# Items of 608 slots instead of 640 in a routed mixture of experts, with places turned into items by comparisons

## The chip, the core and the metric

The program runs on one core of one Trainium2 chip. Its time is the device time of one execution in microseconds (us); the figure that is compared is the median of several executions. TensorE (PE) does the matrix products, VectorE (DVE), ScalarE (ACT) and GpSimd (POOL) the element-wise work, and the queues of SyncE (SP), ACT and POOL issue transfers (DMA).

## The reference, cut to what matters

Three layers follow one another. A linear attention over 4 batches of 576 positions gives 2,304 rows of 512 numbers. A dense layer of hidden width 1,024 with a softmax gate and a norm turns each row into another row `x` of 512. Then a mixture of eight experts takes each row to the one expert with the largest logit:

```python
logits = x @ w_gate
e_idx = np.argmax(logits, axis=1)
...
for e in range(E):                      # E = 8, x is 2304 x 512
    mask = e_idx == e
    if not mask.any():
        continue
    h = np.maximum(x[mask] @ w1[e], 0.0)    # 512 -> 1024
    ye = h @ w2[e]                          # 1024 -> 512
    out[mask] = gate_w[mask, None] * eom[mask, e, None] * ye
```

How many rows an expert gets is known only when the logits are. Everything is float32. The kernel keeps that precision by splitting each operand of the large products into a high and a low half (type fp32r) and adding three products: high by high, high by low, low by high.

## The kernel before, in words

**Tokens.** The 2,304 rows are 18 tiles of 128. For each tile a list of short steps is written (`kp`, `ha`, `ub` and so on), and a long list called `ORDER` fixes by hand the order in which the steps of all tiles are issued. Within that list every instruction of an engine is tied to the one before it on the same engine, so PE, DVE, ACT, POOL and SP each go strictly in the listed order. Behind the list, in the stage of the experts, only PE's order is fixed (`in_turn`); the order on DVE, ACT and POOL is made by a planner that simulates the program when it is built.

**Places.** When the logits of some tiles are there, routing is done for a set of tiles at once (`SETS`: four, four, four, three, two and one tiles, numbered 0 to 5). Step `ra` finds the expert of each token, `rc` and the step `re` (L714 to L745) count how many tokens of the same expert came earlier. That count is the token's `place`. `re` splits it by shift and mask into a block of 128 (`col`) and a lane (`flo`). All of it is DVE work on tiles of 128 by one to four numbers, and each instruction needs the result of the one before. Then `rf` computes the token's weight, `rg` builds for each tile a one-hot matrix of lanes (`ea`) and one of blocks (`er`), and `rh` multiplies the two on PE into a table `tab`: for each expert and each of its blocks, which token sits in which lane. Sets 0 to 4 are in `ORDER`; set 5 is issued behind it, by `rest`.

**Items.** `CAP` = 640 slots make one item: five blocks of 128 (`NBLK`), all of one expert. An expert with more tokens than `CAP` gets further items (up to `NSURE` = 4 of them have columns in the table). Slots without a token are computed too, and their rows are not written. The first `NSURE` = 4 items are always done, unrolled; items beyond that are done in a conditional `body` behind them, if there are any.

For an item, `fetch` gathers rows of `x` by an indirect transfer for each block (L803) and loads the expert's weights. `xpose` transposes the blocks on PE (L158), and ACT and DVE write the high and low halves `xt`. `up` forms the hidden layer: for each of eight groups of 128 hidden units twelve products (four pieces of the width of 512, three each) with a weight block held in PE and the item's slots streaming past. A product streams at most 512 columns, so the slots go in two parts: 256 and 384 for the first item (`up` with `at` 0 and `CA * P`), 320 and 320 for the others. ACT and DVE turn the result into halves `ht` (L929, L930). `down` takes block by block: the block's 128 slots of `ht` are held in PE, and the 512 columns of `w2` stream past, 24 products a block. ACT scales the result (L951), and an indirect transfer scatters the rows to the output (L952).

While an item runs, the weights of the next are loaded and split into halves on ACT, POOL and DVE (`split_behind`), and its blocks are transposed between the products of the last two blocks of `down`. For the first item, two blocks are prepared early (`zg`, `zt`, `zh`, `zs`, inside `ORDER`), and the other three are gathered during its `down` of the first two blocks (`first_item`, L803) and transposed at product group 4 of the second.

All matrix products are recorded at L155, all transposes at L158.

Of the kernel before, what the change touches and what calls it, by code (L numbers as in the profile page):

```python
# [22 lines left out]
F32 = mybir.dt.float32  # L23
F32R = mybir.dt.float32r
I32 = mybir.dt.int32
AF = mybir.ActivationFunctionType
ALU = mybir.AluOpType
# [4 lines left out]
P = 128  # L32
# [4 lines left out]
DM = H * D  # L37
NPAIR = H // 2
# [1 line left out]
NF = F // P  # L40
E = 8
EF = 1024
CAP = 640
NBLK = CAP // P
LT = 4
QA = 3
DF = 4
# [5 lines left out]
NSURE = -(-NT // CAP)  # L53
# [3 lines left out]
NB = NSURE * NBLK  # L57
NR = E * NB
BIG = 8192.0

# [51 lines left out]
def moe_kernel(ctx: ExitStack, tc: tile.TileContext, qT, kT, v, bd, w_in, w_out, g_wg,  # L114
               w1, w2, ident_in, numbers, out):
    nc = tc.nc
# [4 lines left out]
    x2d = dram.tile([NT, DM], F32, name="x2d")  # L121

    ident = cst.tile([P, P], F32, name="ident")
# [26 lines left out]
    def in_turn(ins):  # L150

        return tc.keep_in_program_order(ins) if fixed[0] else ins
# [2 lines left out]
        return in_turn(nc.tensor.matmul(ps, **kw))  # L155

    def transpose(ps, x):
        return in_turn(nc.tensor.transpose(ps, x, ident))  # L158

    def mm3(ps, lh, ll, rh, rl, first, last):  # L160
        mm(ps, lhsT=lh, rhs=rh, start=first, stop=False)
        mm(ps, lhsT=lh, rhs=rl, start=False, stop=False)
        mm(ps, lhsT=ll, rhs=rh, start=False, stop=last)

    with ExitStack() as ab:
# [548 lines left out]
        def re(i):  # L714

            a, z, n, r = named(i)
            d = of["r", i]
            seen = d["seen"]

            base = r("base", [P, 2 * E])  # L720
            V.tensor_copy(out=base, in_=d["pps"])
            total = rt.tile([P, E], F32, tag="total", name=f"total_{a}", bufs=2)
            if count[0] is None:
                V.tensor_copy(out=total, in_=base[:, E:2 * E])
            else:
                V.tensor_tensor(out=total, in0=count[0], in1=base[:, E:2 * E], op=ALU.add)
                V.tensor_tensor(out=base[:, 0:E], in0=base[:, 0:E], in1=count[0], op=ALU.add)
            count[0] = total
            V.tensor_tensor(out=seen, in0=seen, in1=base[:, 0:E].unsqueeze(2).to_broadcast([P, E, n]), op=ALU.add)
            V.tensor_tensor(out=seen, in0=seen, in1=d["oh"], op=ALU.mult)  # L730
            place = r("place", [P, n])
            V.reduce_sum(out=place, in_=seen.rearrange("p e t -> p t e"), axis=AX.X)
            V.tensor_scalar(out=place, in0=place, scalar1=-1.0, scalar2=None, op0=ALU.add)
            pli = r("pli", [P, n], I32)
            V.tensor_copy(out=pli, in_=place)
            plh = r("plh", [P, n], I32)
            V.tensor_scalar(out=plh, in0=pli, scalar1=7, scalar2=None, op0=ALU.arith_shift_right)
            V.tensor_scalar(out=pli, in0=pli, scalar1=127, scalar2=None, op0=ALU.bitwise_and)
            col = d["col"] = r("col", [P, n])
            V.tensor_copy(out=col, in_=plh)  # L740
            flo = d["flo"] = r("flo", [P, n])
            V.tensor_copy(out=flo, in_=pli)

            V.scalar_tensor_tensor(out=col, in0=d["em"][:, :, 0], scalar=-float(NB), in1=col, op0=ALU.mult, op1=ALU.add)
            V.tensor_scalar(out=col, in0=col, scalar1=float(E * NB), scalar2=None, op0=ALU.add)  # L745
# [54 lines left out]
            return o[:, 0:k, 0:b]  # L800

        def gather(x, j, col, n=NT):
            return nc.gpsimd.indirect_dma_start(out=x[:, j, :], out_offset=None, in_=x2d[0:n, :],  # L803
                                                in_offset=bass.IndirectOffsetOnAxis(ap=col, axis=0),
                                                bounds_check=n - 1, oob_is_err=False)

        def load_expert(raw, src, at, eng=nc.sync):
# [20 lines left out]

        def xpose(x, xt, blocks, name):
            for j in blocks:  # L830
                ps = sm.tile([P, NPAIR, P], F32, tag="sm", name=f"xT{name}_{j}")
                for c in range(NPAIR):
                    transpose(ps[:, c, :], x[:, j, c * P:(c + 1) * P])
                hi, lo = (y[:, :, j * P:(j + 1) * P] for y in xt)
                nc.scalar.copy(out=hi, in_=ps)  # L835
                sub(nc.vector, lo, ps, hi)

# [102 lines left out]

    def down(i, ht, blocks, between={}):
        for j in blocks:
            ps = psy.tile([P, DM], F32, tag="psy", name=f"yp{i}_{j}")
            for f in range(EF // P):
                if (j, f) in between:
                    between[j, f]()
                mm3(ps, ht[0][:, f, j * P:(j + 1) * P], ht[1][:, f, j * P:(j + 1) * P],
                    w2h[:, f, :], w2l[:, f, :], f == 0, f == EF // P - 1)
            y = cp.tile([P, DM], F32, tag="y", name=f"y{i}_{j}", bufs=3)
            col = i * NBLK + j  # L950
            nc.scalar.activation(out=y, in_=ps, func=AF.Copy, scale=scs[:, col:col + 1])  # L951
            nc.gpsimd.indirect_dma_start(out=out, out_offset=bass.IndirectOffsetOnAxis(ap=idxs[:, col:col + 1], axis=0),  # L952
                                         in_=y, in_offset=None, bounds_check=NT - 1, oob_is_err=False)

    def new_x(i):
# [193 lines left out]
```

## Time and profile before

| | |
|---|---|
| time, median of 3 runs | 661.83 us (661.37 to 673.13) |
| the profiled execution | 665.99 us, of which its span is 664.3 us |
| granted TensorE clock, mean over the span | 0.983 |
| PE busy | 639.2 us (96% of the span), 4,434 products |
| PE weight loads | 582.0 us (88%) |
| DVE, ACT, POOL busy | 358.8 us, 296.7 us, 163.8 us |
| DMA | 55.22 MB, mean 83 GB/s |

The span runs from the first to the last instruction of the program; times inside it are counted from its start. Products on PE are pipelined: the record of one shows its whole passage, which overlaps the next, so the cost of a product in a stream is the distance from its start to the next start and not its duration. The stage of the experts' items begins at about 417 us; the last 240 us or so are `up` and `down`. The groups of rows on which the prediction rests stand in a section of their own below.

### The profile page before, as it was taken

How to read it: one execution, taken by the hardware profiler on the slowest of the kernel's cores; microseconds unless marked ns; L12 is line 12 of the kernel's file. 1: busy time of each engine (PE TensorE's matmuls, PEld its weight loads, DVE VectorE, ACT ScalarE, POOL GpSimd, SP SyncE). 2: the span in 40 equal slices, each digit the busy share in tenths (PEclk: the TensorE clock that was granted, in tenths of full speed). 3: DMA queues.
4: the chain of work that ended last, by engine and by line, in shares of the span. 5: the costliest groups of instructions: out<-in, count | busy, mean ns of one | idle time of the engine just before them, and what ended most of it. 6: DMA issues, size and time to landing. Idle time of an engine off the chain costs nothing. (4 is left out here: it accounts for less than half of the span.)

```text
span 664.3 us, 11388 instructions
## 1 busy us (share of the span) xinstructions
PE 639.2 (96%) x4434; PEld 582.0 (88%) x4434; DVE 358.8 (54%) x1010; ACT 296.7 (45%) x719; POOL 163.8 (25%) x133
## 2 busy tenths in 40 slices
PE   9988999999999999999999989899999999999995
PEld 8988898899998999889889879779899889889984
DVE  5999977555455446756587586883523222422200
ACT  5677646446435644635424354422443233324210
POOL 1344423111012001110012115044590355216011
PEclk9979969999999999999999999999999999999999
DMA  8952402022210510100000301428542433010001
GB/s 293 303 156 96 143 2 64 1 67 79 65 33 1 159 33 2 33 17 28 6 1 18 143 32 51 156 86 313 181 129 78 165 114 127 17 47 9 1 33 42
DMA packets 35199, 55.22 MB, mean 83 GB/s; under 512 B 2624, under 2 KB 21440, under 8 KB 35137
## 3 DMA queue, kind: packets, MB, share of 16 engines
q1 hardware_dynamic: 28384, 31.73, 14.8%
q0 software_dynamic: 6464, 22.55, 10.0%
q8 instruction: 37, 0.61, 0.4%
q14 instruction: 26, 0.20, 0.1%
q10 hardware_dynamic: 288, 0.13, 0.1%
HBM read 44.96 MB, written 9.96 MB: 83 GB/s over the span
## 5 line engine op out<-in xcount | busy, mean ns | idle before, releaser
L155 PE MATMUL x<-w2h,lth 128*128 128x256 f32 (+1 forms) x288 | 83.8, 291 | 1.4 <-DVE xr L485 1.3
L155 PE MATMUL x<-w2l,lth 128*128 128x256 f32 (+1 forms) x288 | 81.9, 284 | 0.0
L155 PE MATMUL x<-w2h,ltl 128*128 128x256 f32 (+1 forms) x288 | 81.9, 284 | 0.0
L930 DVE SCALAR_TENSOR_TENSOR htl<-hp,hth 128x320 fp32r<-128x320 f32 (+2 forms) x64 | 31.4, 491 | 87.3 <-ACT hth L929 76.8
L558 POOL TENSOR_SCALAR s<-s,st 128x1024 f32<-128x1024 f32 x18 | 23.3, 1294 | 201.9 <-DVE st L554 93.4
L155 PE MATMUL hp<-xth,w1h 128*128 128x320 f32 (+1 forms) x224 | 70.3, 314 | 0.9 <-DVE htl L930 0.9
L155 PE MATMUL hp<-xtl,w1h 128*128 128x320 f32 (+1 forms) x224 | 70.2, 313 | 0.0
L155 PE MATMUL hp<-xth,w1l 128*128 128x320 f32 (+1 forms) x224 | 70.1, 313 | 0.0
L155 PE MATMUL yp<-w2h,hth 128*128 128x512 f32 x160 | 64.2, 401 | 0.0
L155 PE MATMUL yp<-w2l,hth 128*128 128x512 f32 x160 | 63.2, 395 | 0.0
L155 PE MATMUL yp<-w2h,htl 128*128 128x512 f32 x160 | 63.0, 393 | 0.0
L929 ACT ACTIVATE hth<-hp 128x320 fp32r<-128x320 f32 (+2 forms) x64 | 28.1, 439 | 74.4 <-PE hp L155 74.2
L155 PE MATMUL h<-w1h,xth 128*128 128x512 f32 x144 | 58.9, 409 | 0.0
L155 PE MATMUL h<-w1l,xth 128*128 128x512 f32 x144 | 56.9, 395 | 0.0
L155 PE MATMUL h<-w1h,xtl 128*128 128x512 f32 x144 | 56.9, 395 | 0.0
L155 PEld LDWEIGHTS x<-w2h,lth 128*128 128x128 f32 x288 | 54.1, 188 | 2.9 <-issue 1.5
L155 PEld LDWEIGHTS x<-w2l,lth 128*128 128x128 f32 x288 | 54.2, 188 | 0.3
L155 PEld LDWEIGHTS x<-w2h,ltl 128*128 128x128 f32 x288 | 54.3, 189 | 0.0
L525 DVE TENSOR_REDUCE st<-h 128x1 f32<-128x512 f32 x36 | 24.8, 689 | 45.2 <-PE h L155 45.2
L143 DVE TENSOR_TENSOR xtl<-xT,xth 128x512 fp32r<-128x512 f32 x36 | 24.7, 687 | 40.7 <-ACT xth L835 38.2
L372 ACT ACTIVATE qe<-qps,qmx 128x128 f32<-128x128 f32 x144 | 39.0, 392 | 17.1 <-DVE qmx L365 17.1
L951 ACT ACTIVATE y<-yp,scs 128x512 f32<-128x512 f32 x20 | 13.8, 690 | 69.3 <-PE yp L155 61.0
(200 smaller groups left out, 1469.7 us busy)
## 6 DMA issues: line engine op xcount, KB each, us to landing
raw<-in_w POOLq DMA_DIRECT2D x12, 1024.0 KB
v<-in_v SPq DMA_DIRECT2D x18, 260.0 KB, 4.2
kr<-in_kT SPq DMA_DIRECT2D x18, 256.0 KB, 4.5
qr<-in_qT SPq DMA_DIRECT2D x18, 256.0 KB, 4.2
x2d<-xo SPq DMA_DIRECT2D x18, 256.0 KB, 2.0
win<-in_w_in SPq DMA_DIRECT2D x8, 512.0 KB, 7.7
wout<-in_w_out SPq DMA_DIRECT2D x8, 512.0 KB, 3.6
raw<-in_w SPq DMA_DIRECT2D x4, 1024.0 KB, 6.3
```

The lines of the kernel that those rows point to most:

```text
L143: return eng.tensor_tensor(out=out_, in0=a, in1=hi.bitcast(F32), op=ALU.subtract)
L155: return in_turn(nc.tensor.matmul(ps, **kw))
L372: nc.scalar.activation(out=e3[:, 2 * c + j, :], in_=pss[j][:, c, :], func=AF.Exp, bias=nmx[:, j, c:c + 1])
L525: nc.vector.tensor_reduce(out=st[:, n:n + 1], in_=of[f"h{n}", t], axis=AX.X, op=ALU.max, negate=True)
L558: nc.gpsimd.tensor_scalar(out=s, in0=s, scalar1=st[:, 10:11], scalar2=st[:, 11:12], op0=ALU.mult, op1=ALU.add)
L929: act = nc.scalar.activation(out=hi, in_=ps[:, 0:n], func=AF.Relu)
L930: dve = nc.vector.scalar_tensor_tensor(out=lo, in0=ps[:, 0:n], scalar=0.0, in1=hi.bitcast(F32), op0=ALU.max, op1=ALU.subtract)
L951: nc.scalar.activation(out=y, in_=ps, func=AF.Copy, scale=scs[:, col:col + 1])
```

## The change

An item has 608 slots, 19 times 32, instead of 640. There are still five blocks, but the last one holds 96 slots. A new function `slots(j)` gives a block's length, and the gathers, the transposes, the products of `down`, the scaling and the scatters of the last block use 96 partitions or columns instead of 128. In `up` the parts are 256 and 352 for the first item and 304 and 304 for the others. The number of items that are always done (`NSURE`), of items at most (`NITEM`) and of columns in the table (`NR`) come out as before: 4, 11 and 160.

Since a block in the table still has 128 lanes, item k of an expert begins at place 640 k in the table, though its first token is the expert's token 608 k. So 32 is added to a place for each item boundary that it has passed. `re` does that with the place divided by 32: three instructions, one for each k from 1 to 3, compare it with 20 k - 1 and add the comparison's result (1 or 0). The scaling by 1/32 goes into an instruction that was there, and the scaling back replaces a copy.

```diff
-CAP = 640
-NBLK = CAP // P
+CAP = 608
+NBLK = -(-CAP // P)
+SHORT = NBLK * P - CAP
...
+def slots(j):
+    return min(P, CAP - j * P)
...
     def transpose(ps, x):
-        return in_turn(nc.tensor.transpose(ps, x, ident))
+        k = x.shape[0]
+        return in_turn(nc.tensor.transpose(ps, x, ident[0:k, 0:k]))
...
-            V.tensor_scalar(out=place, in0=place, scalar1=-1.0, scalar2=None, op0=ALU.add)
+            V.tensor_scalar(out=place, in0=place, scalar1=-1.0, scalar2=1.0 / SHORT, op0=ALU.add, op1=ALU.mult)
+            for k in range(1, NSURE):
+                V.scalar_tensor_tensor(out=place, in0=place, scalar=float(k * (CAP // SHORT + 1) - 1), in1=place,
+                                       op0=ALU.is_ge, op1=ALU.add)
             pli = r("pli", [P, n], I32)
-            V.tensor_copy(out=pli, in_=place)
+            V.tensor_scalar(out=pli, in0=place, scalar1=float(SHORT), scalar2=None, op0=ALU.mult)
...
         def gather(x, j, col, n=NT):
-            return nc.gpsimd.indirect_dma_start(out=x[:, j, :], out_offset=None, in_=x2d[0:n, :],
-                                                in_offset=bass.IndirectOffsetOnAxis(ap=col, axis=0),
+            k = slots(j)
+            return nc.gpsimd.indirect_dma_start(out=x[0:k, j, :], out_offset=None, in_=x2d[0:n, :],
+                                                in_offset=bass.IndirectOffsetOnAxis(ap=col[0:k], axis=0),
...
         def xpose(x, xt, blocks, name):
             for j in blocks:
-                ps = sm.tile([P, NPAIR, P], F32, tag="sm", name=f"xT{name}_{j}")
+                k = slots(j)
+                ps = sm.tile([P, NPAIR, P], F32, tag="sm", name=f"xT{name}_{j}")[:, :, 0:k]
                 for c in range(NPAIR):
-                    transpose(ps[:, c, :], x[:, j, c * P:(c + 1) * P])
-                hi, lo = (y[:, :, j * P:(j + 1) * P] for y in xt)
+                    transpose(ps[:, c, :], x[0:k, j, c * P:(c + 1) * P])
+                hi, lo = (y[:, :, j * P:j * P + k] for y in xt)
...
     def down(i, ht, blocks, between={}):
         for j in blocks:
-            ps = psy.tile([P, DM], F32, tag="psy", name=f"yp{i}_{j}")
+            k = slots(j)
+            ps = psy.tile([P, DM], F32, tag="psy", name=f"yp{i}_{j}")[0:k]
...
-                mm3(ps, ht[0][:, f, j * P:(j + 1) * P], ht[1][:, f, j * P:(j + 1) * P],
+                mm3(ps, ht[0][:, f, j * P:j * P + k], ht[1][:, f, j * P:j * P + k],
                     w2h[:, f, :], w2l[:, f, :], f == 0, f == EF // P - 1)
-            y = cp.tile([P, DM], F32, tag="y", name=f"y{i}_{j}", bufs=3)
+            y = cp.tile([P, DM], F32, tag="y", name=f"y{i}_{j}", bufs=3)[0:k]
             col = i * NBLK + j
-            nc.scalar.activation(out=y, in_=ps, func=AF.Copy, scale=scs[:, col:col + 1])
-            nc.gpsimd.indirect_dma_start(out=out, out_offset=bass.IndirectOffsetOnAxis(ap=idxs[:, col:col + 1], axis=0),
+            nc.scalar.activation(out=y, in_=ps, func=AF.Copy, scale=scs[0:k, col:col + 1])
+            nc.gpsimd.indirect_dma_start(out=out, out_offset=bass.IndirectOffsetOnAxis(ap=idxs[0:k, col:col + 1], axis=0),
                                          in_=y, in_offset=None, bounds_check=NT - 1, oob_is_err=False)
```

## Rows read from the trace of the kernel before

**Rows 1.** The page: busy time by engine, and the granted clock in 40 slices.
```profile
PE 639.2 (96%) x4434; PEld 582.0 (88%) x4434; DVE 358.8 (54%) x1010; ACT 296.7 (45%) x719; POOL 163.8 (25%) x133
...
PEclk9979969999999999999999999999999999999999
```

**Rows 2.** Windows: window, length, busy of PE, PEld, DVE, ACT, POOL, clock, DMA.
```profile
440.00:640.00 200.00, 198.17 (x1125) 179.75 (x1124) 62.48 (x106) 68.05 (x113) 79.94 (x59) 1.00 0.31 105
```

**Rows 3.** Waits of PE: who waited for whom, total us, times, longest us.
```profile
PE tab L155 <- DVE er L770: 2.8, 3, 1.4
```

**Rows 4.** Groups by line and form, PE: count, busy us, mean ns, idle before.
```profile
L155 PE MATMUL hp<-xth,w1h 128*128 128x320 f32 x192 | 59.5, 310 | 0.9 <-DVE htl L930 0.9
...
L155 PE MATMUL kv<-v,ke 128*128 128x65 f32 x256 | 30.7, 274 | 0.0
...
L155 PE MATMUL kv<-v,ke 64*128 64x65 f32 x64 | 9.1, 300 | 0.0
```

**Rows 5.** Timeline of PE (start us, duration us): first and last of three streams.
```profile
305.90 0.28 PE L155 MATMUL x<-w2h,lth 128*128 128x256 f32 x1
...
308.63 0.28 PE L155 MATMUL x<-w2h,ltl 128*128 128x256 f32 x1
...
600.58 0.31 PE L155 MATMUL hp<-xth,w1h 128*128 128x320 f32 x1
...
628.73 0.40 PE L155 MATMUL yp<-w2h,hth 128*128 128x512 f32 x1
...
656.29 0.40 PE L155 MATMUL yp<-w2h,htl 128*128 128x512 f32 x1
```

**Rows 6.** Timeline of DVE and PE, set 3 of the routing; idle before in brackets.
```profile
391.14 0.17 DVE L733 TENSOR_SCALAR place<-place 128x3 f32<-128x3 f32 x1
391.35 0.17 DVE L735 CAST pli<-place 128x3 int32<-128x3 f32 x1
...
394.76 0.71 DVE L770 SCALAR_TENSOR_TENSOR er<-nums,col,tsc 128x480 fp32r<-128x480 f32 x1
...
395.53 0.71 PE L155 MATMUL tab<-er,ea 128*128 128x480 f32 x2 [1.36 <-DVE er L770]
```

**Rows 7.** Timeline of DVE and PE behind set 4, where the items begin.
```profile
419.12 0.69 DVE L143 TENSOR_TENSOR xtel<-xTe,xteh 128x512 fp32r<-128x512 f32 x1
...
419.86 0.39 PE L155 MATMUL hp<-xtel,w1h 128*128 128x256 f32 x1 [2.32 <-DVE xtel L143]
```

**Rows 8.** Timeline of DVE and PE behind set 2.
```profile
345.38 0.71 DVE L770 SCALAR_TENSOR_TENSOR er<-nums,col,tsc 128x480 fp32r<-128x480 f32 x1
...
346.42 0.38 PE L155 MATMUL tab<-er,ea 128*128 128x480 f32 x1
```

**Rows 9.** Timeline of DVE behind sets 0 and 1, idle before in brackets.
```profile
274.38 0.69 DVE L525 TENSOR_REDUCE st<-h 128x1 f32<-128x512 f32 x1 [0.57 <-PE h L155]
...
311.43 0.69 DVE L143 TENSOR_TENSOR ltl<-lT,lth 128x512 fp32r<-128x512 f32 x1 [3.35 <-ACT lth L586]
```

**Rows 10.** Timeline of DVE and PE behind set 5.
```profile
431.04 0.71 DVE L770 SCALAR_TENSOR_TENSOR er<-nums,col,tsc 128x480 fp32r<-128x480 f32 x1
...
434.45 0.38 PE L155 MATMUL tab<-er,ea 128*128 128x480 f32 x1
```

**Rows 11.** Timeline of POOL and PE: the first item's last gather and its transposes.
```profile
439.91 1.00 POOL L803 DMA_INDIRECT xg<-x2d,idxg  x1 [0.30 <-issue]
...
443.72 0.63 PE L158 MATMUL xT<-ident,xg 128*128 128x128 f32 x4 [0.97 <-DVE idxg L984]
```

**Rows 12.** The last scatter: POOL's timeline, then the DMA view 657.7:664.3 (packets, MB).
```profile
657.79 0.98 POOL L952 DMA_INDIRECT out_y<-y,idxs  x1 [4.63 <-ACT y L951]
...
q0 software_dynamic: 80, 0.10, 4.7%
```

**Rows 13.** Windows, columns as in the second group: one at half clock, one around 419.86.
```profile
82.00:95.00 13.00, 12.75 (x65) 12.17 (x66) 9.99 (x29) 7.12 (x18) 1.30 (x1) 0.50 0.07 24
...
412.00:422.00 10.00, 7.68 (x66) 7.47 (x65) 8.24 (x56) 2.75 (x9) 0.00 (x0) 1.00 0.55 201
```

## The prediction

> **What bounds the kernel now.** I read the page first. PE is busy for 639.2 us of a span of 664.3, no other engine for more than 54% of it, and outside two early dips the granted clock is full [rows 1]. In the stage of the items the window view says the same more sharply: 198.17 of 200 us [rows 2]. So time falls there only by what leaves PE's own stream, and time rises wherever PE is made to wait longer. The waits of PE say where it waits for DVE on the way to the items: three times for the one-hot matrix `er` of the routing, 2.8 us together [rows 3], and once, for 2.32 us, for the low half of the first item's transposed rows [rows 7]. Those are the places where added DVE work can show.
>
> What a product costs PE I take from starts in undisturbed streams, not from the records' durations [rows 5]. 24 products of 256 columns start from 305.90 to 308.63, 23 steps of 118.7 ns. 192 of 320 columns start from 600.58, and what follows them starts at 628.73: 146.6 ns. 120 of 512 columns start from 628.73 to 656.29, 119 steps of 231.6 ns. Between 256 and 320 columns that is 0.436 ns a column, between 320 and 512 it is 0.443. I take 0.44.
>
> **The products of `up`.** Items 1 to 3 have 576 products in all of 320 columns (three operand pairs, one row each of 192 [rows 4]); each loses 16. The first item has 96 of 384 columns; each loses 32. That is 576 x 16 + 96 x 32 = 12,288 columns, at 0.44 ns **5.4 us less** (5.36 to 5.44 by the two slopes). All of it lies on PE's path, because PE stands still for 1.83 of 200 us there [rows 2]. ACT and DVE, busy for about a third of that window, have shorter operands to evict and nothing more to do. The weights' splits get 1.35 us less cover per `up`; POOL, the busiest of them, has 120 of 200 us idle there, so I cost that at nothing (if that cover fails, at most the same 1.35 us per item comes back, 5.4 in all).
>
> One rule can be set beside this. The Trainium skill, "TensorE: Matmul & The Clock Gate", section "Back-to-back issue gap", gives the distance of warm products as the columns at 2.4 GHz plus about 2.5 ns. By it 320 columns would take 135.8 ns, where this trace has 146.6, and the 12,288 columns would be worth 5.1 us, an estimate from that page, so that the whole sum would come out 0.3 us smaller.
>
> **The last block in `down`.** The number of products stays at 24 a block, 96 for the four last blocks, and the streamed operand stays at 512 columns; only the held one has 96 columns instead of 128. In rows 5 the distance follows the streamed columns with 128 held throughout; a product with 96 held is in no row. If the held share counted fully, 96 products would lose a quarter of 231.6 ns: 5.6 us of gain. On the other side stands the nearest pair of rows with a partly filled array: products of 65 columns take 274 ns with all 128 rows of the array and 300 ns with 64 [rows 4], though there the filled rows differ and not the held columns; 26 ns for each of 96 products would be 2.5 us of loss. I take 0, since the streamed columns alone account for the three distances to within 2%. The transposes of last blocks, 96 rows instead of 128, go with this: the first item's four take 0.63 us together [rows 11], so for four items a quarter is 0.6 us at most; I take 0.
>
> **The three comparisons.** Each set of tiles gets three more dependent DVE instructions on a few numbers; the two instructions that change form keep their place. The step from one such instruction to the next that needs it is 391.14 to 391.35, 0.205 us [rows 6], so a set's chain grows by 0.61 us. What that does differs by set, since DVE goes in a fixed order in sets 0 to 4:
> - Set 0: DVE idles 0.57 us a little later, for PE [rows 9], which takes up nearly all. Set 1: it idles 3.35 us before the next tile's lower half [rows 9]. Cost 0 each, 0.61 each if those covers were gone.
> - Set 2: `er` ends at 346.09, PE takes it at 346.42 [rows 8]. Where PE waits for `er`, it starts 0.06 us after its end (394.76 + 0.71 to 395.53 [rows 6]), so 0.27 us are spare: **+0.3**.
> - Set 3: PE already waits 1.36 us for the `er` that follows it in DVE's order [rows 6]. Behind it the table, the first item's gather and every later DVE step move too, but PE moves with them: **+0.6**.
> - Set 4: its steps stand ahead of `xtel` in DVE's order, and PE waits 2.32 us for that [rows 7]: **+0.6**.
> - Set 5: the planner weaves it between evictions and splits. Its `er` ends at 431.75 and PE comes to it at 434.45 [rows 10]. 2.7 us of cover against 0.61 us, or some 2 us if each new instruction falls behind a larger one: 0.
>
> Together **+1.5 us**; bounds 0 (the planner hides it all) and 6 x 0.61 = 3.7.
>
> **The short transfers.** POOL issues as many gathers and scatters as before, the last of each item for 96 rows. Those of items 1 to 3 run far ahead of their use; with 56 us an item (192 x 146.6 ns and 120 x 231.6 ns [rows 5]) for five of each, they have time enough, and I cost them at 0; without that time they would arrive earlier by up to a quarter of a transfer, a gain. Two are on the path. The first item's last gather is issued at 439.91, and PE waits 0.97 us for its rows at 443.72 [rows 11]: a quarter fewer rows of a transfer of 3.8 us is 0.95 at most, 0 at least; a fixed part and the scatter beside it keep most of that, so **-0.3**. Once 0.97 us are gone, the product stream itself is late next, so no more than that can be had. The very last scatter takes POOL 0.98 us [rows 12], and again a quarter is the most; I take **-0.1**.
>
> **Sum.** -5.4 + 1.5 - 0.3 - 0.1 = -4.3 us. The profiled execution, 665.99 us with a span of 664.3, would become 661.7. It stands 4.2 us above the median of 661.83, about as much as the whole change is worth, so I apply the sum to the median: **657.5 us**.
>
> **Rivals.** *The comparisons cost nothing.* PE may be late at the three places by other means, or the planner may fill the holes with set 5. Then -5.8: 656.0 us. Against it: in all three places PE's wait ends with DVE's instruction. Chance 0.12.
>
> *The clock falls* (the case that ends slower). The wait at 419.86 is the longest of PE's waits for DVE and grows to 2.9 us. If the granted clock drops there from its upper level, 2.4 GHz, to half, the products that follow cost double. In 82 to 95 us the clock was 0.50 for 13 us [rows 13], 6.5 us lost; the third slice of the page, 0.7 of 16.6 us, lost 3.3 to 5.0 [rows 1]. So 660.8 to 664.0 us, slower than before from a fall of more than 8.6 us on. Against it: with 2.32 us of wait the clock was 1.00 throughout 412 to 422 us [rows 13]. Chance 0.08. The same page of the Trainium skill, in "Why this matters for your kernels", warns of idle gaps of TensorE between bursts, because the clock then goes back to half; no run here shows it at this place.
>
> *The held columns count.* -4.3 - 5.6: 651.9 us. For it speaks only that no row excludes it. Chance 0.05; that the short block costs instead, 2.5 us more and 660.0, 0.05.
>
> *A fifth item* (the change does not do what it says). With more than 608 tokens in one expert, `body` runs. An item takes 56 us, so 713 us or more. The reference, evaluated on its drawn inputs, gives 561, 576, 576 and 591 tokens to four experts and none to the others, and the trace's last scatter moved 0.10 MB [rows 12], which at 2 KB a row is 49 rows, 561 less 512. 17 tokens are left before it decides. Chance 0.02.
>
> **The numbers.** The forecast has 0.65, and 0.03 are left for an order of the planner that I don't see. The range: the bounds of the comparisons (up to 2.2 us more), of the gather and the scatter (0.8 less, 0.4 more) and 1.4 us for one uncovered split put the forecast's own range at 655 to 661; it reaches down to 653.5 and up to 664.5 to take in most of the rivals and a spread of the runs. What a measurement of this kernel can tell from no change is about 2%, 13 us: below 648.6 lies only something unseen (0.03), above 675.1 the fifth item and as much again unseen (0.05).
>
> **What would show it.** Right: products of 304 columns about 139.5 ns apart and those of 352 about 160.7; those of the last block with 96 held still about 232; PE's waits for `er` near 395.5 and for `xtel` near 420 longer by 0.6 us each; a new wait of 0.3 us behind set 2; the wait before the first item's last transposes near 0.7 us. Wrong: distances that do not follow the columns, the waits unchanged, a clock below 1.00 after 420 us, or a wait of PE for `w1` or `w2` halves in the items.

## The result and the profile after

The changed kernel takes 656.15 us (median of 4 runs, 655.86 to 669.36); the kernel before had a median of 667.1 in four runs, the first three of which are those with the median of 661.83. The ratio is 0.9916, 95% interval 0.9887 to 0.9945: a gain of 5.7 us against 661.83, less than the 2% from which a result counts as different from no change. The forecast was 657.5. Executions of every kernel here, the one before included, come in groups by their mean granted clock (before: mostly 661 to 666 us at 0.983 to 0.990, or 670 to 677 at 0.962 to 0.971), so medians of few runs mix them; below, executions at like clock and stages of traces are compared.

The page of the changed kernel, its span, busy times and granted clock, the last to be read against [rows 1]:

```profile
span 654.0 us, 11406 instructions
...
PE 628.1 (96%) x4434; PEld 567.9 (87%) x4434; DVE 360.3 (55%) x1028; ACT 295.0 (45%) x719; POOL 163.3 (25%) x133
...
PEclk9979999999999999999999999999999999999999
```

The number of products is unchanged, and DVE has 18 more instructions, three for each of six sets. The second dip of the clock, in slice 6 of [rows 1], is not there. It is 82 to 95 us in [rows 13], long before anything that the change touches. The profiled execution of before stood 4.2 us above its median, that of the changed kernel, 655.86 us, stands at its median. The two spans differ by 10.3 us, and 4.4 of that lie ahead of a product of the table `tab` at 343.40 us before and 338.96 after, which stands ahead of the first wait that the comparisons lengthen. So only somewhat more than half of it can belong to the change.

The starts of `up` and `down` in the timeline of PE, changed kernel (start us, duration us), which answer to [rows 5]:

```profile
443.36 0.32 PE L162 MATMUL hp<-xth,w1h 128*128 128x352 f32 x1
...
458.66 0.39 PE L162 MATMUL yp<-w2h,hth 128*128 128x512 f32 x1
...
591.56 0.30 PE L162 MATMUL hp<-xth,w1h 128*128 128x304 f32 x1
...
618.34 0.40 PE L162 MATMUL yp<-w2h,hth 128*128 128x512 f32 x1
...
645.65 0.39 PE L162 MATMUL yp<-w2h,hth 128*96 128x512 f32 x1
...
646.12 0.40 PE L162 MATMUL yp<-w2h,htl 128*96 128x512 f32 x1
```

192 products of 304 columns take 26.78 us, 139.5 ns each; 96 of 352 take 15.30 us, 159.4 ns each. The prediction named 139.5 and 160.7. The products with 96 columns held, at the end, still start 0.23 to 0.24 us apart. By form, products and weight loads of the last blocks:

```profile
L162 PE MATMUL yp<-w2h,hth 128*96 128x512 f32 x32 | 13.0, 406 | 0.0
...
L162 PEld LDWEIGHTS yp<-w2l,hth 128*96 128x96 f32 x32 | 5.2, 162 | 1.9
```

One thing was not foreseen: the last `down` takes 27.78 us (618.34 to 646.12) where [rows 5] has 27.56.

DVE and PE behind sets 2 and 3 and where the items begin, changed kernel, to be read against [rows 6 to 8] (idle before in brackets):

```profile
341.53 0.71 DVE L782 SCALAR_TENSOR_TENSOR er<-nums,col,tsc 128x480 fp32r<-128x480 f32 x1
...
342.30 0.49 PE L162 MATMUL tab<-er,ea 128*128 128x480 f32 x1 [0.16 <-DVE er L782]
...
387.19 0.17 DVE L742 TENSOR_SCALAR place<-place 128x3 f32<-128x3 f32 x1
...
387.98 0.17 DVE L747 TENSOR_SCALAR pli<-place 128x3 int32<-128x3 f32 x1
...
391.39 0.71 DVE L782 SCALAR_TENSOR_TENSOR er<-nums,col,tsc 128x480 fp32r<-128x480 f32 x1
...
392.16 0.48 PE L162 MATMUL tab<-er,ea 128*128 128x480 f32 x1 [1.95 <-DVE er L782]
...
416.36 0.68 DVE L150 TENSOR_TENSOR xtel<-xTe,xteh 128x512 fp32r<-128x512 f32 x1
...
417.09 0.39 PE L162 MATMUL hp<-xtel,w1h 128*128 128x256 f32 x1 [2.90 <-DVE xtel L150]
```

From the first `place` to the conversion it is now 0.79 us, where [rows 6] had 0.21: 0.58 us for three comparisons. PE's wait grows by 0.59 us behind set 3 and by 0.58 before the items, and behind set 2 a wait of 0.16 us is new. From the product of the table behind set 2 to the first of the items it is now 74.79 us (342.30 to 417.09) where it was 73.44 (346.42 in [rows 8] to 419.86 in [rows 7]), and the product behind set 2 itself comes 0.32 us later after the one ahead of it (3.34 us instead of 3.02): together PE reaches the items 1.67 us later by the comparisons. PE's waits, for [rows 3], four now instead of three:

```profile
PE tab L162 <- DVE er L782: 3.6, 4, 2.0
```

The first item's last gather and its transposes, POOL and PE of the changed kernel, for [rows 11]:

```profile
436.42 1.33 POOL L816 DMA_INDIRECT xg<-x2d,idxg  x1 [0.30 <-issue]
...
439.35 0.30 PE L166 MATMUL xT<-ident,xg 128*128 128x128 f32 x1 [0.59 <-DMA xg<-x2d,idxg]
...
440.17 0.55 PE L166 MATMUL xT<-ident,xg 96*128 96x96 f32 x4 [0.19 <-DVE xtl L150]
```

The wait of 0.97 us became two of 0.59 and 0.19; from the start of the last gather to the transposes of its block it is 3.75 us (436.42 to 440.17) where [rows 11] has 3.81. The last scatter, for [rows 12], takes POOL 0.92 us instead of 0.98:

```profile
647.56 0.92 POOL L967 DMA_INDIRECT out_y<-y,idxs  x1 [4.60 <-ACT y L966]
```

### The profile page after: what moved, and what is told of

It reads as the page before. It is cut to its first block, busy times and chain, and to the rows that moved or that the text cites. A ratio compares the mean times of both kernels' runs of the same rounds, so it can differ in the third digit from the quotient of the medians.

```text
span 654.0 us, 11406 instructions
## 1 busy us (share of the span) xinstructions
PE 628.1 (96%) x4434; PEld 567.9 (87%) x4434; DVE 360.3 (55%) x1028; ACT 295.0 (45%) x719; POOL 163.3 (25%) x133
## 4 chain that ended last, share of the span: by engine, by line
PE 71%; DVE 12%; issue 6%; DMA 5%; POOL 2%; ACT 2%; SPq 0%; POOLq 0%; DVEq 0%
PE x L162 14%; PE hp L162 13%; PE yp L162 13%; PE h L162 13%; PE kv L162 3%; PE num L162 3%; PE xT L166 2%; PE qps L162 2%; DMA out_y<-y,idxs 2%; PE kps L162 2%; PE lT L166 2%; PE qT L166 2%; DMA win<-in_w_in 1%; DMA wout<-in_w_out 1%; DVE xr L493 1%
## 5 line engine op out<-in xcount | busy, mean ns | idle before, releaser
L944 DVE SCALAR_TENSOR_TENSOR htl<-hp,hth 128x304 fp32r<-128x304 f32 (+2 forms) x64 | 30.3, 474 | 81.2 <-ACT hth L943 66.9
L162 PE MATMUL hp<-xth,w1h 128*128 128x304 f32 (+1 forms) x224 | 68.5, 306 | 0.0
L162 PE MATMUL hp<-xtl,w1h 128*128 128x304 f32 (+1 forms) x224 | 68.4, 305 | 0.0
L162 PE MATMUL hp<-xth,w1l 128*128 128x304 f32 (+1 forms) x224 | 67.9, 303 | 0.0
L162 PE MATMUL yp<-w2h,hth 128*128 128x512 f32 (+1 forms) x160 | 64.1, 401 | 0.0
L162 PE MATMUL yp<-w2h,htl 128*128 128x512 f32 (+1 forms) x160 | 63.5, 397 | 0.0
L162 PE MATMUL yp<-w2l,hth 128*128 128x512 f32 (+1 forms) x160 | 63.4, 396 | 0.0
L943 ACT ACTIVATE hth<-hp 128x304 fp32r<-128x304 f32 (+2 forms) x64 | 27.2, 424 | 68.3 <-PE hp L162 68.2
L150 DVE TENSOR_TENSOR xtl<-xT,xth 128x512 fp32r<-128x512 f32 (+1 forms) x36 | 24.1, 672 | 40.6 <-ACT xth L849 38.0
L966 ACT ACTIVATE y<-yp,scs 128x512 f32<-128x512 f32 (+1 forms) x20 | 13.8, 688 | 70.3 <-PE yp L162 62.0
```

What stands on the lines that cost most here:

```text
L150: return eng.tensor_tensor(out=out_, in0=a, in1=hi.bitcast(F32), op=ALU.subtract)
L943: act = nc.scalar.activation(out=hi, in_=ps[:, 0:n], func=AF.Relu)
L944: dve = nc.vector.scalar_tensor_tensor(out=lo, in0=ps[:, 0:n], scalar=0.0, in1=hi.bitcast(F32), op0=ALU.max, op1=ALU.subtract)
```

## The experiments

Two theories stood against each other at first. Theory A is the prediction's sum: the columns give 5.4 us, the comparisons take 1.5 back. Theory B is its first rival: the comparisons cost nothing, and the whole gain of 5.7 is columns.

**Both kernels again.** No edit. First the changed one:

> The changed kernel once more, as the base for the others. Main theory: the columns of `up` give 5.4 us, the comparisons take 1.4 us back at sets 2, 3 and 4, the short transfers give 0.3 us, and PE's short waits early in `up` of items 1 and 2 (0.45 and 0.41 us before) are gone, about 0.9 us: 5.2 us less than before, ratio 0.992. Rival: the comparisons cost nothing and the waits are chance: 5.7 us less, 0.9914. PE waits again 1.9 to 2.0 us near 392 and 2.9 us near 417.

Median 665.22 us (656.20 to 668.64) beside 670.85 of before (661.17 to 676.51), ratio 0.9984 [0.9893, 1.0075]. At a clock of 0.99 it took 656.20, where before took 661.17 to 661.89 at 0.988 and 0.989: the 5 to 6 us are there again. The trace, of an execution at 0.967, has the same waits as the first (0.16, 1.94, 2.91 us) and `up` of 26.78 us for each of items 1 to 3; in the first trace items 1 and 2 had 27.03 and 26.95.

> The kernel before once more, for a second trace. Theory that the clock's second early dip of the first trace (81 to 95 us) is chance: this trace may lack it, and then PE comes to the first product of the items some 3 to 4 us earlier than at 417.26. Theory that the waits of 0.45 and 0.41 us early in `up` of items 1 and 2 belong to the program: both are there again; rival that they are chance: one or both are gone and `up` takes 28.15 us in all three items.

673.81 us, clock 0.968. Half clock was granted in three stretches of some 10 us each within the first 100 here, where the first trace had two, of 7 and 14. So the dips are not the same from execution to execution, but PE comes to the items later than the 417.26 us of the first trace, at 424.78, where the theory had it 3 to 4 us earlier. `up` takes 28.15 to 28.16 us in items 1 to 3, as the rival had it. The first trace of before had 28.86 and 28.83 in items 1 and 2 and 28.15 in item 3; the two longer ones hold waits of 0.4 us that come and go between executions of one kernel. So the clean gain is 28.16 - 26.78 = 1.38 us an item.

**The columns put back.** The changed kernel, with comparisons and short `down` kept:

```diff
         def gather(x, j, col, n=NT):
-            k = slots(j)
+            k = P
...
         def xpose(x, xt, blocks, name):
...
-                k = slots(j)
+                k = P
...
-        return [cp.tile([P, NPAIR, CAP], F32R, tag=f"xt{k}", ...
+        return [cp.tile([P, NPAIR, NBLK * P], F32R, tag=f"xt{k}", ...
...
-        return [cp.tile([P, EF // P, CAP], F32R, tag=f"ht{k}", ...
+        return [cp.tile([P, EF // P, NBLK * P], F32R, tag=f"ht{k}", ...
...
-    up(0, xt, ht, CA * P, CAP - CA * P)
+    up(0, xt, ht, CA * P, NBLK * P - CA * P)
...
-        up(i, xt, ht, 0, CAP // 2, ...        # and the second half
+        up(i, xt, ht, 0, NBLK * P // 2, ...
```

> `up` streams 640 slots again (256 and 384, 320 and 320), and gathers and transposes take full last blocks; `down` and the scatter keep the short last block, and the comparisons stay. Main theory: the whole gain of the columns goes and the comparisons' cost stays, so 1.4 us slower than before if the early waits in `up` return, 0.5 us if they don't: ratio 1.001 to 1.002. Rival that held columns count: still 4 to 5 us faster than before, 0.993. Rival that the comparisons cost nothing: 1.000.

673.52 us (660.84 to 677.03), ratio 0.9970 [0.9864, 1.0077]; at clocks of 0.991 and 0.994 661.15 and 660.84, against 655.86 to 656.44 of the changed kernel at 0.990 to 0.993. Beside the kernel before, at 661.17 to 661.89, that is no loss, where the main theory had one of 0.5 to 1.4 us. Its trace, timeline of PE:

```profile
443.44 0.34 PE L162 MATMUL hp<-xth,w1h 128*128 128x384 f32 x1
...
460.33 0.39 PE L162 MATMUL yp<-w2h,hth 128*128 128x512 f32 x1
...
479.22 0.31 PE L162 MATMUL hp<-xth,w1h 128*128 128x320 f32 x1
...
507.38 0.39 PE L162 MATMUL yp<-w2h,hth 128*128 128x512 f32 x1
...
651.27 0.39 PE L162 MATMUL yp<-w2h,htl 128*96 128x512 f32 x1
```

Up to the items this trace agrees with that of the changed kernel (second item product at 416.98 and 417.09); the last product is 5.15 us later. `up` takes 16.89 and 28.16 us, as before the change. All of that difference arises behind the start of the items.

**The comparisons taken out, and the comparisons alone.** First the changed kernel without them (all tokens still come out, as no expert has more than 608):

```diff
-            for k in range(1, NSURE):
-                V.scalar_tensor_tensor(out=place, ..., op0=ALU.is_ge, op1=ALU.add)
```

> The changed kernel without the three comparisons; it leaves out the shift of places past an item boundary. Main theory: PE's waits behind sets 3 and 4 go back to 1.36 and 2.32 us and the one behind set 2 vanishes: 1.4 us faster than the changed kernel, ratio to before 0.990. Rival that the comparisons are hidden: the same time as the changed kernel within 0.2 us, waits or no waits.

665.60 us (656.01 to 669.39), ratio 0.9983 [0.9876, 1.0090]. PE's waits in its timeline are those of before to the hundredth:

```profile
350.85 0.38 PE L162 MATMUL tab<-er,ea 128*128 128x480 f32 x1
...
399.95 0.49 PE L162 MATMUL tab<-er,ea 128*128 128x480 f32 x1 [1.35 <-DVE er L779]
...
424.28 0.39 PE L162 MATMUL hp<-xtel,w1h 128*128 128x256 f32 x1 [2.32 <-DVE xtel L150]
```

From the table behind set 2 to the items it takes 73.43 us, as before the change. Yet its execution at a clock of 0.990 took 656.01 us, no less than the changed kernel's 655.86 to 656.44. The kernel before with nothing but the scaling and the comparisons:

```diff
-            V.tensor_scalar(out=place, in0=place, scalar1=-1.0, scalar2=None, op0=ALU.add)
+            SHORT, SLOTS = 32, 608
+            V.tensor_scalar(out=place, in0=place, scalar1=-1.0, scalar2=1.0 / SHORT, op0=ALU.add, op1=ALU.mult)
+            for k in range(1, NSURE):
+                V.scalar_tensor_tensor(out=place, in0=place, scalar=float(k * (SLOTS // SHORT + 1) - 1), in1=place,
+                                       op0=ALU.is_ge, op1=ALU.add)
...
-            V.tensor_copy(out=pli, in_=place)
+            V.tensor_scalar(out=pli, in0=place, scalar1=float(SHORT), scalar2=None, op0=ALU.mult)
```

Items keep their 640 slots.

> The kernel before with the scaling and the three comparisons alone, thresholds of 608 and a shift of 32; items keep 640 slots (no expert of these inputs passes a threshold, so places stay). Main theory: 1.4 us slower than before; PE's wait behind set 3 is 1.95 us, the one before the items 2.9 us, and one of 0.15 to 0.3 us comes behind set 2. Rival that the planner hides them: waits of 1.36 and 2.32 us and the same time.

672.47 us (661.03 to 674.18), ratio 0.9995 [0.9901, 1.0089]; its two executions at 0.991 took 661.03 and 661.51, the seven of before beside it at 0.986 to 0.989 took 660.96 to 661.77. Timeline of PE:

```profile
351.20 0.48 PE L155 MATMUL tab<-er,ea 128*128 128x480 f32 x1 [0.16 <-DVE er L774]
...
401.03 0.48 PE L155 MATMUL tab<-er,ea 128*128 128x480 f32 x1 [1.95 <-DVE er L774]
...
427.14 0.39 PE L155 MATMUL hp<-xtel,w1h 128*128 128x256 f32 x1 [2.90 <-DVE xtel L143]
```

So both theories were half right. The waits of theory A are there and come from the comparisons; the times of theory B are there too. These fastest executions were not the ones traced (those of the two kernels took 664.22 and 670.99 us), so what each of them lost elsewhere is not on record. In the traces a part that can give the 1.5 us back shows in the stretch from the second item product to the first of `down`, about 101 products in each kernel. Windows (columns as in [rows 2]), first the kernel before in its third trace:

```profile
417.00:431.10 14.10, 14.01 (x101) 13.64 (x102) 10.76 (x30) 6.50 (x11) 0.00 (x0) 0.88 0.28 105
```

The changed kernel without comparisons:

```profile
424.30:438.30 14.00, 14.00 (x101) 13.68 (x102) 10.91 (x30) 6.49 (x11) 0.00 (x0) 0.88 0.29 107
```

The changed kernel:

```profile
417.10:429.50 12.40, 12.40 (x101) 12.26 (x102) 10.73 (x33) 6.49 (x11) 0.00 (x0) 1.00 0.26 100
```

The kernel before with the comparisons alone:

```profile
427.20:439.50 12.30, 12.30 (x101) 12.19 (x102) 10.65 (x33) 6.49 (x11) 0.00 (x0) 1.00 0.28 104
```

PE is busy nearly throughout in all four. Without comparisons the granted clock averages 0.88 over 14.1 us: 1.7 us lost, which is half clock for 3.4 us, within 1 us behind the wait of 2.32 us. With them, behind a wait of 2.90 us, it is 1.00.

This is one place of two. The stretch ahead of it, from the table behind set 3 to the first item product, has 172 products in both kernels with comparisons. Windows, the changed kernel and then the kernel before with the comparisons alone:

```profile
392.16:417.09 24.93, 21.72 (x172) 20.87 (x172) 19.28 (x80) 8.66 (x18) 9.25 (x6) 1.00 0.27 90
```

```profile
401.03:427.14 26.11, 23.19 (x172) 22.18 (x172) 17.08 (x80) 8.66 (x18) 9.29 (x6) 0.93 0.27 84
```

The trace with the comparisons alone has a fall of 3.4 us too, 25 us earlier, and loses 1.2 us by it. So it does not show that comparisons come free: from the table behind set 2 to the items it takes 75.94 us, which is the 74.79 of the changed kernel and these 1.2.

**The last block whole.** In `gather`, `xpose` and `down` the last block gets 128 again, for which the rows of `xt` have 640 numbers (`down` holds slots 480 to 607 for it, so rows of its output are in part other tokens' rows):

```diff
-            k = slots(j)
+            k, b = P, min(j * P, CAP - P)
...
-                mm3(ps, ht[0][:, f, j * P:j * P + k], ht[1][:, f, j * P:j * P + k],
+                mm3(ps, ht[0][:, f, b:b + k], ht[1][:, f, b:b + k],
...
-        return [cp.tile([P, NPAIR, CAP], F32R, tag=f"xt{k}", ...
+        return [cp.tile([P, NPAIR, NBLK * P], F32R, tag=f"xt{k}", ...
```

> `up` streams 608 slots as in the changed kernel, but gathers, transposes, `down` and scatters take a last block of 128; `down` holds slots 480 to 607 for it, so the last block's rows are computed from other slots. Main theory: 0.2 to 0.4 us slower than the changed kernel (the first item's last gather and the last scatter), ratio to before 0.9925. Rival that the 96 held columns or the short transfers carry the gain: 4 to 5 us slower than the changed kernel, ratio 0.999 to 1.000.

665.77 us (656.79 to 669.42), ratio 0.9992 [0.9901, 1.0083]; at a clock of 0.992 656.79, 0.4 to 0.9 us more than the changed kernel. Timeline of PE:

```profile
601.42 0.30 PE L162 MATMUL hp<-xth,w1h 128*128 128x304 f32 x1
...
628.09 0.39 PE L162 MATMUL yp<-w2h,hth 128*128 128x512 f32 x1
...
655.92 0.40 PE L162 MATMUL yp<-w2h,htl 128*128 128x512 f32 x1
```

The last `down` takes 27.83 us with 128 held throughout, 27.78 with 96 in its last block. With rows of 640 in `ht` the two widths agree as well: 27.56 with 128 in [rows 5], 27.56 with 96 in the kernel with the columns put back. The held columns do not count. `up` takes 26.67 here, 0.11 less than in the changed kernel; that was explained only by the last experiment.

**What decides whether the clock falls behind the items' wait.** Theory: the length of that wait (2.32 us falls, 2.90 does not). Rival: where the wait stands. Comparisons in set 4 alone make the wait long, comparisons in all other sets leave it short. The kernel before ran beside them, unchanged, for a third trace:

```diff
-            for k in range(1, NSURE):
+            for k in range(1, NSURE if i == 4 else 1):     # first kernel
+            for k in range(1, 1 if i == 4 else NSURE):     # second kernel
```

> The kernel before, for a trace of a fast execution. Theory that part of the measured gain is the clock's: this trace shows a fall to half clock of 3.4 us right behind the wait of 2.32 us before the items, which the changed kernel's traces don't have there; the stretch from the second product of the items to the first of `down` takes 14.1 to 14.4 us. Rival: no fall there, some 13.2 us, and the whole gain is the kernel's own work.

> The changed kernel with the three comparisons in set 4 alone; it leaves out the shift of places of the other sets. Theory that the longer wait itself (2.9 us) keeps the clock up: no fall behind it, waits behind sets 2 and 3 as before the change, 0.9 us less than the changed kernel, 655.0 us in executions with one early dip. Rival that it is the place of the wait in time: a fall of 3.4 us behind it and 656.6 us.

> The changed kernel with the comparisons in all sets but set 4; it leaves out the shift of places there. Theory that the length of the wait before the items decides: it is 2.32 us, a fall of 3.4 us follows, 1.1 us more than the changed kernel, 656.9 us with one early dip. Rival that only the DVE steps count: 0.6 us less than the changed kernel, 655.3 us, no fall.

Before: 662.91 us (661.87 to 664.73), ratio 0.9976 [0.9868, 1.0084]. Set 4 alone: 668.89 (664.09 to 671.46), 1.0056 [0.9980, 1.0133], no execution above a clock of 0.978. The others: 667.41 (658.32 to 670.30), 1.0001 [0.9884, 1.0117]. The waits in the timeline of PE, comparisons in set 4 alone:

```profile
427.81 0.39 PE L162 MATMUL hp<-xtel,w1h 128*128 128x256 f32 x1 [2.91 <-DVE xtel L150]
```

Comparisons in the other sets, the wait and then the window behind it:

```profile
418.00 0.39 PE L162 MATMUL hp<-xtel,w1h 128*128 128x256 f32 x1 [2.32 <-DVE xtel L150]
```

```profile
418.00:430.40 12.40, 12.40 (x101) 12.28 (x102) 10.74 (x33) 6.50 (x11) 0.00 (x0) 1.00 0.33 120
```

A wait of 2.32 us, and no fall, as in the first trace of before: the length alone does not decide, and the theory as put has fallen. The rival is not shown by that either. Over all traces, the last experiment's included, the fall behind the items' wait is there in 5 of 7 with a wait of 2.31 to 2.52 us and in 0 of 7 with one of 2.90 or 2.91; counted by edit, in 5 of 6 without any comparison and in 0 of 8 with comparisons in some set. Behind the table of set 3 it is rather the other way round. A fall of the same length is there in 4 of 7 traces with a wait of 1.94 or 1.95 us and in 2 of 7 with one of 1.35 to 1.55; by edit, in 5 of the 8 with comparisons and in 1 of the 6 without, the second trace of before, which has both falls. It costs 1.1 to 1.2 us up to the items where the wait is the longer one, and 1.6 where it is not. So with comparisons the fall stands earlier in five traces and is absent in three; that longer waits keep the clock up in general is not so.

**Another way to the item number, and smaller items.** The item is found by one multiplication whose rounding to an integer does the comparing:

```diff
+            V.tensor_scalar(out=past, in0=place, scalar1=1.0 / CAP, scalar2=-0.5 - 0.5 / CAP, op0=ALU.mult, op1=ALU.add)
+            V.tensor_scalar(out=place, in0=place, scalar1=-1.0, scalar2=None, op0=ALU.add)
+            V.scalar_tensor_tensor(out=pli, in0=past, scalar=float(SHORT), in1=place, op0=ALU.mult, op1=ALU.add)
```

It stands in place of the scaling, the three comparisons and the scaling back (`past` and `pli` are int32). The second kernel has `CAP = 592` besides; the largest expert has 591 tokens.

> The changed kernel with the item's number from one multiplication and a rounding to an integer instead of three comparisons (place less one is formed beside it). The chain from the place's sum to its integer has two dependent steps as before the change. Main theory: PE's waits go back to 1.4 and 2.4 us, so 1.2 us faster than the changed kernel at an equal clock, 6.5 less than before, ratio 0.990. Rival: no change against the changed kernel.

667.71 us (657.97 to 668.91), ratio 0.9999 [0.9929, 1.0069]. The waits are 1.55 and 2.51 us, 0.4 shorter than with three comparisons, but the fall behind the items' wait is back (427.8 us, 3.4 us long), and no gain of 1.2 us can be seen.

> As the one-conversion kernel, with items of 592 slots (the largest expert has 591 tokens). Main theory, columns times 0.44 ns: products of 296 columns 136 ns apart, of 336 columns 153 to 154 ns; 6,144 columns less, so 2.7 us faster than with 608, 9 us less than before, ratio 0.986. Rival: a floor under the distance or a block of 80 slots that costs more, so no gain over 608; a fifth item would make it some 55 us slower.

659.29 us (653.79 to 665.67), ratio 0.9892 [0.9773, 1.0010]; 653.79, 654.24 and 655.09 at clocks of 0.984 to 0.989, among them the fastest execution of all kernels here. Against the 660.96 to 661.77 of before at 0.986 to 0.989 that is 6 to 8 us less, where the theory had 9. Timeline of PE:

```profile
443.64 0.32 PE L162 MATMUL hp<-xth,w1h 128*128 128x336 f32 x1
...
458.49 0.39 PE L162 MATMUL yp<-w2h,hth 128*128 128x512 f32 x1
...
590.67 0.30 PE L162 MATMUL hp<-xth,w1h 128*128 128x296 f32 x1
...
616.85 0.40 PE L162 MATMUL yp<-w2h,hth 128*128 128x512 f32 x1
```

136.4 ns for 296 columns, 154.7 for 336: the slope goes on. Its products of `down` stand 231.6 to 231.9 ns apart in all four items. In the changed kernel the four means are 232.5, 232.9, 232.9 and 233.5, in the other traces with rows of 608 in `ht` within about 0.4 ns of that, and in the kernel with the columns put back, whose tiles have rows of 640, 231.6 to 232.1.

**The row length.** So the changed kernel with nothing but longer rows in the tiles of `xt` and `ht`:

```diff
-        return [cp.tile([P, NPAIR, CAP], F32R, tag=f"xt{k}", ...
+        return [cp.tile([P, NPAIR, NBLK * P], F32R, tag=f"xt{k}", ...
-        return [cp.tile([P, EF // P, CAP], F32R, tag=f"ht{k}", ...
+        return [cp.tile([P, EF // P, NBLK * P], F32R, tag=f"ht{k}", ...
```

> The changed kernel, and the tiles of transposed rows (xt) and of the hidden layer (ht) have rows of 640 numbers instead of 608; the last 32 are not used, and every instruction keeps its size. In the traces so far the products of down stand 231.6 to 231.9 ns apart where ht has rows of 640 or 592 numbers (the kernel before, the one with wide up, the one of 592 slots) and 232.9 to 233.5 ns where it has rows of 608, whatever the held width. Theory that the row length of the tile sets this: down at 231.6 to 231.9 ns in all four items, the last down 27.56 us instead of 27.78; up at 138.9 ns a product instead of 139.5, as it was with xt of 640 beside slots of 608; together 0.12 + 2 x 0.13 + 0.22 for down and 576 x 0.6 ns = 0.35 for up, 0.7 to 0.95 us less than the changed kernel at like clock (655.0 to 655.5 where that showed 655.9 to 656.2). Rival, that the shorter products of up or the changed scheduling behind them do it: down stays at 232.9 to 233.5 and the last down at 27.78, up at 139.5, 0.0 us.

664.44 us (654.67 to 668.64), ratio 0.9940 [0.9830, 1.0050]; 654.67 at a clock of 0.991, 1.2 to 1.8 us less than the changed kernel at 0.990 to 0.993, from one execution. The trace, of another execution (664.39 us), first the 352 columns of the first item:

```profile
452.33 0.33 PE L162 MATMUL hp<-xth,w1h 128*128 128x352 f32 x1
...
468.35 0.39 PE L162 MATMUL yp<-w2h,hth 128*128 128x512 f32 x1
...
600.27 0.30 PE L162 MATMUL hp<-xth,w1h 128*128 128x304 f32 x1
...
626.93 0.39 PE L162 MATMUL yp<-w2h,hth 128*128 128x512 f32 x1
...
654.50 0.39 PE L162 MATMUL yp<-w2h,htl 128*96 128x512 f32 x1
```

`up` takes 26.66 us and the last `down` 27.57, with distances of 138.8 and 231.6 ns. The rival, that the shorter `up` does it, is out. Rows of 608 numbers cost the changed kernel 0.12 us in each of three `up`, and about 0.5 in the four `down` (109 x 1.2 ns twice, 119 x 1.9 once, little in the first). But the 96 products of 352 columns take 16.02 us here, 166.9 ns each, where the two traces of the changed kernel have 15.30 and 15.47 and the kernel with the whole last block, with rows of 640 in `xt` alone, 15.31. Why is not known, and it takes back 0.5 to 0.7 of the 0.85 us. Longer rows also move the tiles that lie behind them in memory; that the place of a tile and not its row length counts was not tried. That this version is faster than the changed kernel rests on one execution.

## Why the prediction was nearly right, point by point

The direction, the size class and every wait it named came as written; the time was 1.35 us below the forecast, inside the range. That it fell inside is luck in part: run again, the same kernel had a median of 665.22, above the range of 653.5 to 664.5, and about 1 us of the measured gain is not in the sum.

- **Columns, -5.4.** Clean stages give 1.60 (16.90 to 15.30) and three times 1.38: 5.7 us. The distance for 304 columns came as named, with some luck: with rows of 640 it is 138.8 to 138.9, and the row length adds the rest. That for 352 is 159.4 and not 160.7, and that for 384, which had not been read, is 176.0 where the same line has 174.8; the row for 352 was 161.1 in the second trace and 166.9 with longer rows, so this width does not keep to one line. The Trainium skill, "TensorE: Matmul & The Clock Gate", section "Back-to-back issue gap", would put 304 columns at 129.2 ns, an estimate from that page; the trace has 139.5.
- **Comparisons, +1.5.** As waits: 0.32 at set 2 (from table to table 3.02 to 3.34 us), 0.59 at set 3, 0.58 before the items, 0 at sets 0, 1 and 5; together 1.5. Taking them out and putting them in alone moves exactly these waits, and in traces without a fall up to there PE reaches the items 1.6 to 1.7 us later with them. **In the whole time the step does not show:** the fastest executions with and without comparisons agree (656.0 and 655.9 to 656.4; 661.0 to 661.5 and 661.0 to 661.8). It assumed that all behind the items' wait would be equal before and after, and it read that from the one trace of before, of three, that has no fall there [rows 13]. From the first item product to the last product it is 236.43, 236.26 and 237.78 us in the three traces of before, and 234.31 with the comparisons alone, where neither waits in `up` nor a fall took anything in that stretch.
- **The clock.** The rival had a fall appear behind the items' wait when it grew; instead a fall of 1.7 us is seen there in five traces behind the shorter wait and in none behind the longer, the opposite of what I priced. But with comparisons a fall stands behind set 3 in 5 of 8 traces, a place that the rival did not name. The same page of the Trainium skill, in "Why this matters for your kernels", warns of idle gaps between bursts; the prediction said no run showed it here. Five traces now show a fall at this place, all behind waits of 2.31 to 2.52 us and none behind one of 2.90, which the warning would not tell.
- **Held columns, 0.** Right, to 0.05 us over a last `down` (27.78 with 96, 27.83 with 128; 27.56 for both with longer rows). Their weight loads are shorter (162 ns instead of 188) and hidden. The rivals of 651.9 and 660.0 are out.
- **Transposes, 0 with a bound of 0.6.** 96x96 ones start 82 ns apart, 128x128 ones 109: 16 x 27 ns = 0.4 us of gain. I took the lower end and was off by that much.
- **Gather -0.3, scatter -0.1.** The first item's stage from first `yp` to the second part of `up` took 13.91, 14.01 and 14.17 us in the three traces of before and 13.79 and 14.18 in the two of the changed kernel, part of it the transposes; the tail behind the last product 8.04, 8.34 and 8.13, then 7.91 and 8.14. Not contradicted, but of a size that single traces do not settle.
- **Not in the sum:** the row length, +0.5 in `down`.

Adding the stages: +1.5 - 0.4 - 5.7 - 0.1 + 0.3 - 0.2 = -4.6 us of the program's own, where the forecast had -4.3 (the 0.1 is the first item's second part of `down`, 18.95 to 18.84; the 0.3 is all other `down`). Other pairs of traces give other values for the 0.4 and the 0.2, down to nothing, and the 1.5 is 1.7 by the stages. The measured 5.7 holds about 1.1 us more. Two things could make that up. One is the fall behind the items, 1.7 us; that the executions without a trace had it is argued from their lower clock (before at 0.986 to 0.990, comparisons alone 0.991), not shown. The other is the waits early in `up` of items 1 and 2, which come and go: they lengthen `up` by 1.4 us in the first trace of before and by 0.4 in the first of the changed kernel, where neither has the fall, and by 2.1 in each of the two kernels with comparisons in some sets only. The record does not say which it was in the executions of the result. So 656.15 lies at the rival "the comparisons cost nothing" (656.0), but not by its mechanism.

What decides the fall stays open. The comparisons also move the waits against the start of the program by a few tenths of a microsecond; whether this is what counts was not tried.

## What to carry to other kernels

A stream's cost per column, taken from starts in two streams of different width, carried to a third width within 0.1 ns where that lay between the two; 352 columns were off by 1.3. An added wait is not added time until the stage behind it has been looked at in several executions: one trace does not tell whether a short fall of the clock is part of the kernel's usual run, and a fall that is gone from one stage may stand in the stage ahead of it. And when a size changes, look at the row length of the tiles as well as at the work: here rows of 608 instead of 640 took back 0.85 us in `up` and `down` of some 6, though the longer rows lost most of that again in one stream.

## What was not expected of the hardware

- Products that hold or stream from tiles with rows of 608 numbers of 4 bytes stand 1.2 to 1.9 ns (held, 512 columns) and 0.7 ns (streamed, 304 columns) further apart than with rows of 640; with rows of 592 the held case shows 0 to 0.3. The stream of 352 columns does not fit in: 159.4 and 161.1 ns with rows of 608, 166.9 with rows of 640. Why is not known.
- At half clock products of 256 columns stand 213 ns apart, at full clock 118.7: less than double.
- Early in `up` of items 1 and 2 PE waits 0.4 to 0.9 us in some executions and not in others of the same kernel (none in the second trace of before, 0.50 and 0.44 in the third). PE, third trace of before:

```profile
486.33 0.31 PE L155 MATMUL hp<-xth,w1l 128*128 128x320 f32 x1
487.14 0.42 PE L155 MATMUL hp<-xth,w1h 128*128 128x320 f32 x1 [0.50 <-DVE htl L930]
```

The products before it ran at their usual distance, and the eviction that frees the buffer began late. Its cause was not found.
